# Block-causal attention and a token and channel mixer: u in one buffer, its float16 parts in two, with a new order

## Chip, cores and metric

The kernel runs on one core of a Trainium2 chip. The metric is the device time of one execution in microseconds. Engines: PE is the matrix engine (PEld its weight loads), DVE, ACT and POOL the vector, scalar and general engines, SP the engine whose queue issues all DMAs here.

## The reference

Eight batches of eight heads, 576 tokens, head size 64. The attention is masked by blocks of 64 tokens (a token sees its own block and those before). Its output, all heads beside each other, is x (8 x 576 x 512), and a mixer follows:

```python
theta = x @ w_theta
zr, zi = x * np.cos(theta), x * np.sin(theta)
y = np.einsum('ts,bsd->btd', w_tok_r, zr) + np.einsum('ts,bsd->btd', w_tok_i, zi)
u = x + y
return u + np.maximum(u @ w_ch, 0.0)
```

Inputs and outputs are float32. The kernel reaches that precision on PE by splitting operands into two 16-bit (or reduced float32) parts and adding three products: high by high, low by high, high by low.

## The kernel before

A pair p is two heads; four pairs make one batch b. For each pair the scores go into PSUM in three pieces (parts sab, sc, sd), DVE takes row maxima (m), ACT the exponentials (e), ACT and DVE split them into two float16 parts (high, low), a DMA transposes them (turn), PE multiplies with v (weighted), and DVE divides by the sums (normalise). Pairs 0 to 3 go another way: PE transposes the float32 exponentials (tp), ACT or DVE copies them (cp), and v is scaled in float32 (vf, the function v_scaled).

For each batch the mixer takes x through these parts: xh, xl, xt split and turn x; theta is a product on PE; turns, rest, size, sines make cosine and sine; z multiplies them with x; zh and zl are the float16 parts of z; mix is the token product on PE, 27 matmuls of 288 columns for each of 4 blocks of 128 channels (dt) and 2 halves of the tokens (th). The rest is about u:

- xs (add_parts, L837) adds the two x parts into u for two dt at once (dp 0 or 1), on DVE; xd (unscale, L841, run by the helper `times`, L319 on ACT and L323 on DVE) scales them;
- u (take_u, L845) adds the mix result from its PSUM bank, in place;
- uh (L851, helper) and ul (L856) make the float16 parts of u in the tile uhl;
- c (channel, L865) multiplies them with the channel weights, 12 matmuls for each of 4 dt (called e) and 2 halves;
- out (rectify, L871) adds the rectified result to u, in place; fin (unlift) rescales u, in place; store (L880) writes u out by a DMA from SP's queue.

u lies in two buffers, used by turns: `u_all[self.b % 2]`. uhl has one buffer. The first u buffer first holds the identity (`made_ident`), the second the float32 channel weights before they are split (L373). The uhl buffer first holds raw weights (L368).

The order is written out. Each part has its needs: `turn_of(tag, last, bufs)` hands a part the users of the buffer's former content. The list PLACES gives each part a place; `order_of` sorts the parts by it and asserts that all needs come first. Instructions are issued in that order, so each engine's queue follows it. Two needs matter here: mix of batch b needs all c of batch b-1 (L1059), and uh needs the last reader of its uhl buffer (L1050). ON names, with a letter for each instance, the engine of a part (P is POOL, D is DVE, A is ACT). BANKS gives the PSUM banks in the order in which parts take them: bank 0 is the attention output o, banks 1 to 7 go to scores, theta, mix (group y) and c. RUNNING places filler matmuls on ones (L1082): before the n-th part of the order, into a bank, so many.

Of the kernel before, what the change touches and what calls it, by code (L numbers as in the profile page):

```python
# [181 lines left out]


RUNNING = [
    (12, 0, 7), (25, 0, 13), (43, 0, 8), (63, 0, 3), (75, 0, 3), (336, 0, 3), (396, 3, 8), (404, 5, 2), (767, 1, 5)
]
ON = {"w5": "AAAAAAAAA",
      "wc": "PDDDPPPDP",
      "vc": "DPDPPPPDPDDPPPDPPPPPPPDP",
      "qh": "APPPPAPPPAPPPAAPAAAAPPPAPAAPPAAA",  # L190
      "vf": "PDDD",
      "cp": "DDDADDAADAAAADAA",
# [943 lines left out]
```

## Time and profile before

| what | value |
|---|---|
| median of 3 runs | 674.82 us (672.94 to 677.4) |
| the profiled execution | 670.92 us, of it 669.1 us span |
| PE, DVE, ACT, POOL busy | 97%, 86%, 79%, 26% of the span |
| granted clock of PE | 1.0 of full speed |

The profile shows one execution. The span runs from the first to the last instruction; busy is the time in which an engine had an instruction under way, and for PE the ends of matmuls are modelled, since they overlap. "Releaser" of an idle time is what ended it.

### The profile page before, as it was taken

What the parts mean: (1) busy time and instruction counts of PE and PEld (TensorE: products, weight loads), DVE (VectorE), ACT (ScalarE), POOL (GpSimd) and SP (SyncE); (2) the same over time, 40 slices, a digit from 0 to 9 for tenths busy, and PEclk for the clock granted to TensorE, in tenths of its full rate; (3) what the DMA queues carried; (4) which work ended last, traced back from release to release, by engine and by line L of the source; (5) the groups of instructions that cost most, each with busy time, mean ns of one, the idle gap of its engine ahead of it and who ended that gap; (6) DMA issues with size and microseconds to landing.
All of it is one profiled execution on the core that took longest, in us unless ns stands there. A gap on an engine that the chain in (4) does not pass through costs nothing.

```text
span 669.1 us, 17391 instructions
## 1 busy us (share of the span) xinstructions
PE 649.4 (97%) x7285; PEld 501.6 (75%) x7285; DVE 575.9 (86%) x844; ACT 531.5 (79%) x829; POOL 176.4 (26%) x214
## 2 busy tenths in 40 slices
PE   8899999999989999999999999999999999999997
PEld 4688856887658767887688867888678867886675
DVE  5999899899898989999999999889999999755534
ACT  5999798877898689896997699887898799737611
POOL 1302313211042004640072003340183003611600
PEclk9999999999999999999999999999999999999999
DMA  8871265998989977799779787879989753950101
GB/s 330 321 295 65 90 126 109 215 217 201 225 173 192 203 169 143 185 193 241 170 155 186 167 191 167 179 165 180 196 168 201 166 102 96 194 85 19 54 1 72
DMA packets 245854, 110.51 MB, mean 165 GB/s; under 512 B 227216, under 2 KB 227216, under 8 KB 245776
## 3 DMA queue, kind: packets, MB, share of 16 engines
q1 hardware_dynamic: 245776, 109.40, 72.9%
q8 instruction: 57, 0.93, 0.6%
q14 instruction: 21, 0.17, 0.1%
HBM read 43.06 MB, written 9.44 MB: 78 GB/s over the span
## 4 chain that ended last, share of the span: by engine, by line
PE 62%; ACT 14%; DVE 10%; DMA 8%; issue 3%; POOL 1%; SPq 0%; ACTq 0%; DVEq 0%; POOLq 0%
PE ps L832 25%; PE ps L763 10%; PE ps L865 9%; PE ps L673 9%; PE ps L589 7%; DMA pt<-p 5%; DVE m L623 4%; ACT t L627 3%; ACT p L319 2%; DMA q<-in_qT 2%; DVE p L654 2%; ACT aa L797 1%; ACT zh L317 1%; DMA w_raw<-in_w_theta 1%; PE ps L602 1%
## 5 line engine op out<-in xcount | busy, mean ns | idle before, releaser
L627 ACT ACTIVATE t<-ps,m 128x320 f32<-128x320 f32 (+4 forms) x320 | 149.1, 534 | 32.6 <-DVE m L623 23.8
L832 PE MATMUL ps<-wT_h,zh 128*128 128x288 f16 x540 | 154.7, 286 | 1.3 <-ACT t L627 0.9
L832 PE MATMUL ps<-wT_h,zl 128*128 128x288 f16 x540 | 154.4, 286 | 1.3 <-DVE zl L822 1.1
L832 PE MATMUL ps<-wT_l,zh 128*128 128x288 f16 x540 | 154.4, 286 | 0.0
L623 DVE TENSOR_REDUCE m<-ps 128x2 f32<-128x896 f32 (+4 forms) x160 | 125.0, 816 | 14.4 <-PE ps L594 9.0
L832 PEld LDWEIGHTS <-zh 128*128 128x128 f16 x1080 | 105.5, 98 | 27.4 <-issue 0.9
L673 PE MATMUL ps<-v,pt 128*128 128x65 f16 (+1 forms) x2760 | 114.2, 200 | 3.2 <-DMA pt<-p 1.3
L654 DVE SCALAR_TENSOR_TENSOR p<-t,p 128x1664 f16<-128x1664 f32 x56 | 105.6, 1898 | 6.2 <-ACT p L319 6.1
L865 PE MATMUL ps<-uhl,wch_h 128*128 128x288 f16 x512 | 95.3, 286 | 0.2 <-DVE u L871 0.2
L319 ACT ACTIVATE p<-t 128x1664 f16<-128x1664 f32 x56 | 88.3, 1606 | 2.8 <-DMA pt<-p 2.3
L673 PEld LDWEIGHTS <-pt 128*128 128x128 f16 x2520 | 82.1, 97 | 8.5 <-DMA pt<-p 3.8
L763 PE MATMUL ps<-wth_h,xt 128*128 128x512 f16 (+1 forms) x384 | 87.5, 345 | 0.1
L763 PEld LDWEIGHTS <-xt 128*128 128x128 f16 (+1 forms) x576 | 46.5, 102 | 44.7 <-issue 3.0
L865 PE MATMUL ps<-uhl,wch_l 128*128 128x288 f16 x256 | 73.2, 286 | 0.0
L832 PEld LDWEIGHTS <-zl 128*128 128x128 f16 x540 | 52.8, 98 | 15.8 <-DVE zl L822 2.0
L865 PEld LDWEIGHTS <-wch_h 128*128 128x128 f16 x512 | 48.6, 98 | 14.5 <-issue 1.3
L763 PE MATMUL ps<-wth_l,xt 128*128 128x512 f16 (+1 forms) x192 | 57.3, 344 | 0.0
L589 PE MATMUL ps<-k,qh 64*128 64x288 f32 (+3 forms) x384 | 50.0, 395 | 3.0 <-POOL qh L540 1.9
L809 POOL TENSOR_TENSOR aa<-aa,x_ring 128x512 f32<-128x512 f32 (+1 forms) x29 | 36.2, 1257 | 54.0 <-ACT aa L799 24.9
L589 PEld LDWEIGHTS ps<-k,qh 64*128 64x128 f32 x384 | 34.8, 189 | 16.7 <-issue 3.5
L845 DVE SCALAR_TENSOR_TENSOR u<-ps,gain,u 128x288 f32<-128x288 f32 x64 | 31.5, 511 | 17.1 <-PE ps L832 16.6
L822 POOL TENSOR_TENSOR zl<-aa,zh 128x512 f16<-128x512 f32 (+1 forms) x26 | 28.0, 1079 | 48.8 <-ACT zh L317 48.6
(165 smaller groups left out, 1150.6 us busy)
## 6 DMA issues: line engine op xcount, KB each, us to landing
raw_v<-in_v SPq DMA_DIRECT2D x32, 384.0 KB, 4.3
q<-in_qT SPq DMA_DIRECT2D x32, 320.0 KB, 3.6
k<-in_kT SPq DMA_DIRECT2D x32, 320.0 KB, 3.6
out<-u SPq DMA_DIRECT2D x32, 288.0 KB, 2.4
w_raw<-in_w_tok SPq DMA_DIRECT2D x5, 576.0 KB, 6.0
p<-in_w_tok SPq DMA_DIRECT2D x4, 576.0 KB, 6.0
w_raw<-in_w_theta SPq DMA_DIRECT2D x2, 512.0 KB, 6.4
p<-in_w_theta SPq DMA_DIRECT2D x2, 512.0 KB, 8.3
```

The source lines that it names most:

```text
L319: engine.mul(to, x, scale)
L589: nc.tensor.matmul(s[hh][:, col:col + n], lhsT=qq[rows, i * P:(i + 1) * P], rhs=kk[rows, k0:k0 + n], start=nn == 0 and (j == 0 or c == "ab ...
L623: nc.vector.tensor_reduce(out=m, in_=s, axis=AX.XY if i in (2, 3) else AX.X, op=ALU.max, negate=True)
L627: nc.scalar.activation(out=to, in_=s, func=AF.Exp, scale=1.0, bias=m)
L654: nc.vector.scalar_tensor_tensor(out=self.p[:, 1, :], in0=self.t, scalar=LIFT, in1=self.p[:, 0, :], op0=ALU.mult, op1=ALU.subtract)
L673: nc.tensor.matmul(o[:, i, :], lhsT=pp[:, block, :], rhs=vv[:, of, hh, :], start=nn == 0, stop=nn == n - 1)
L763: nc.tensor.matmul(g[rows, 0:cols.stop - cols.start], lhsT=x[:, dt, part, i, rows], rhs=ww[:, dt, cols], start=(n == 0), stop=(n == 11))
L809: engine_of("z", (2 * self.b + hf) * 5 + n).tensor_tensor(out=cd, in0=cd, in1=x, op=ALU.mult)
L822: engine_of("zl", (2 * self.b + hf) * 5 + n).tensor_tensor(out=zl, in0=cv, in1=zh, op=ALU.subtract)
L832: nc.tensor.matmul(g, lhsT=zz[:, kk, cols], rhs=ww[:, kk, ts], start=(n == 0 and kk == k0 and nn == 0), stop=(n == 4 and nn == 2))
L845: nc.vector.scalar_tensor_tensor(out=self.u(dt)[:, ts], in0=bank("y", self.b, dt, th)[:, 0:HS], scalar=g_y, in1=self.u(dt)[:, ts], op0=ALU ...
L865: nc.tensor.matmul(g[:, 0:HS], lhsT=ww[:, dt, e * P:(e + 1) * P], rhs=uu[:, dt, th * HS:(th + 1) * HS], start=(n == 0), stop=(n == 11))
```

## The change

u has one buffer for all batches. uhl has two, named uhl0 and uhl1, used by turns. The channel weights and the identity share the one u buffer, the raw weights take uhl0. Through `turn_of`, xs of batch b now needs the stores of batch b-1 instead of b-2 (batch 0 needs the last split of the channel weights), and uh of batch b needs c of batch b-2 instead of b-1. The rule that mix of batch b needs c of batch b-1 stays. PLACES, BANKS, RUNNING and parts of ON are written anew.

```diff
 RUNNING = [
-    (12, 0, 7), (25, 0, 13), (43, 0, 8), (63, 0, 3), (75, 0, 3), (336, 0, 3), (396, 3, 8), (404, 5, 2), (767, 1, 5)
+    (11, 0, 7), (24, 0, 12), (65, 0, 5), (78, 0, 2), (336, 0, 3), (381, 0, 5), (392, 1, 5), (399, 1, 2), (767, 1,
+    4)
 ]
 ON = {"w5": "AAAAAAAAA",
...
-      "qh": "APPPPAPPPAPPPAAPAAAAPPPAPAAPPAAA",
-      "vf": "PDDD",
-      "cp": "DDDADDAADAAAADAA",
+      "qh": "APAPPPPAAPPAPPAPPAAPPPPAPAAPPAPP",
+      "vf": "PPPP",
+      "cp": "DDDADAAAADAAAAAA",
...
-      "z": "DDDDDPDDPDPDDDDPPDDPDDPPPPDPPDPPDPDDDPDPPDPPDPPPPDDPPDDPDPDPDPPPPPPPPPPPDDPPDPPP",
+      "z": "PDPPDDPDDDPPDPPDDDPDDDPPPPPPDPPPDPPPDDDPPDPDPPDDPPPDPDDDDDPDPDPPPPDDDPPDDDPPDPDD",
...
-      "zl": "DPPPPPPDPDPDDDPPDDDPPPPPDPPPPDPPDDPDDDPDPDDDPPPPPDPPPDPPPPDPPPDPDDPDDPPDDDDPPPDP",
+      "zl": "PDPDPDPPPPPDDDPDPDDDPPDPPPDPPPPPPPDPPPDPDDPPPPPDPPDDPDPPPDPPDPPPDPPDDPPPPDDDPPP",
...
-      "xd": "DDADADAAAAADADAA",
+      "xd": "DDDDAAAAAAAADDAA",
       "uh": "AAAAAAAAAAAAAAAA",
-      "fin": "PDPDPPPPPAADADAPPPAPDADAADDDDDDPDAAAADD"}
+      "fin": "AAPDPDAAADAADDAAPAPADDPPPDDADDDDADDDDADP"}
...
-    u_all = [const.tile([P, NDT, S], F32, name=f"u{i}") for i in range(2)]
-    made_ident = u_all[0][:, 0, 0:P]
+    u_all = const.tile([P, NDT, S], F32, name="u_all")
+    made_ident = u_all[:, 0, 0:P]
...
-    raws = [mo.tile([P, 2, 2 * S], U32, tag="uhl", name="w_raw"),
+    raws = [mo.tile([P, 2, 2 * S], U32, tag="uhl0", name="w_raw"),
...
-            "ch": u_all[1][:, :, 0:DM]}
+            "ch": u_all[:, :, 0:DM]}
...
         def u_parts(self):
-            both = self.tile_of("uhl", [P, 2, NDT, S], F16)
+            both = self.tile_of(f"uhl{self.b % 2}", [P, 2, NDT, S], F16)
...
         def u(self, dt):
-            return u_all[self.b % 2][:, dt]
+            return u_all[:, dt]
...
     for dp in range(NDT // 2):
-        turn_of(f"u{dp}", [w_last["ch"][dp]], 2)
+        turn_of(f"u{dp}", [w_last["ch"][dp]])
...
-        u_free = turn_of("uhl", c_all)
+        u_free = turn_of(f"uhl{b % 2}", c_all)
         for dp in range(NDT // 2):
             two = (2 * dp, 2 * dp + 1)
-            free = turn_of(f"u{dp}", [("store", b, dt) for dt in two], 2)
+            free = turn_of(f"u{dp}", [("store", b, dt) for dt in two])
```

## Rows read from the trace of the kernel before

**Rows 1.** The page: the span, and busy us (share) xinstructions by engine.
```profile
span 669.1 us, 17391 instructions
...
PE 649.4 (97%) x7285; PEld 501.6 (75%) x7285; DVE 575.9 (86%) x844; ACT 531.5 (79%) x829; POOL 176.4 (26%) x214
```

**Rows 2.** Four stretches: length, busy us by engine, PE clock, DMA share, GB/s.
```profile
0.00:100.00 100.00, 90.91 (x772) 70.74 (x773) 86.26 (x135) 86.53 (x138) 21.89 (x61) 1.00 0.61 205
100.00:260.00 160.00, 154.72 (x1799) 115.14 (x1796) 144.67 (x212) 134.69 (x210) 29.19 (x34) 1.00 0.91 189
260.00:660.00 400.00, 398.67 (x4682) 311.88 (x4681) 342.39 (x493) 309.51 (x482) 124.81 (x120) 1.00 0.71 146
660.00:669.10 9.10, 5.07 (x42) 3.82 (x39) 2.57 (x6) 0.78 (x2) 0.51 (x1) 0.98 0.34 130
```

**Rows 3.** The chain that ended last, its tail: start us, us, what.
```profile
621.66 5.18 PE ps L763 x24
626.84 26.46 PE ps L832 x216
653.30 11.77 PE ps L865 x96
```

**Rows 4.** Tile uhl: what its engines' idle time ended with (us, times).
```profile
  DVE u L845: 16.5, 4
  ACT uhl L319: 5.0, 6
  DVE u L871: 0.2, 1
```

**Rows 5.** Waits of PE, one of them: us in total, times, longest.
```profile
PE ps L832 <- DVE u L871: 0.4, 1, 0.4
```

**Rows 6.** Tile u: count, ns min/median/max, first and last start; landing of stores last.
```profile
L837 DVE TENSOR_TENSOR u<-xt x16: 1342/1348/1355, 82.0 to 602.6; 128x1152 f32<-128x1152 f16 x16
L319 ACT ACTIVATE u<-u,gain x10: 1238/1257/1289, 144.9 to 604.0; 128x1152 f32<-128x1152 f32 x10
L323 DVE TENSOR_SCALAR u<-u,gain x6: 810/814/821, 83.4 to 554.5; 128x1152 f32<-128x1152 f32 x6
L425 DVE SCALAR_TENSOR_TENSOR wch_l<-u,size_ch,wch_h x2: 1274/1280/1285, 69.9 to 71.5; 128x1024 f16<-128x1024 f32 x2
...
DMA to landing us min/median/max: 2.1/2.4/6.8
```

**Rows 7.** Timelines of SP and DVE: stores and the next batch's first u.
```profile
348.86 2.32 SPq L880 DMA_DIRECT2D out<-u  x2
354.60 0.50 DVE L845 SCALAR_TENSOR_TENSOR u<-ps,gain,u 128x288 f32<-128x288 f32 x1
500.94 0.38 SPq L880 DMA_DIRECT2D out<-u  x1
509.94 0.52 DVE L845 SCALAR_TENSOR_TENSOR u<-ps,gain,u 128x288 f32<-128x288 f32 x1
575.82 0.57 SPq L880 DMA_DIRECT2D out<-u  x1
584.24 0.94 DVE L845 SCALAR_TENSOR_TENSOR u<-ps,gain,u 128x288 f32<-128x288 f32 x2
```

**Rows 8.** Lines 569 and 809: count, ns min/median/max, first and last start.
```profile
L569 DVE TENSOR_SCALAR v<-raw_v,sizes x3: 611/612/612, 30.1 to 48.7; 128x768 f32<-128x768 f32 x3
L569 POOL TENSOR_SCALAR v<-raw_v,sizes x1: 1895/1895/1895, 25.4 to 25.4; 128x768 f32<-128x768 f32 x1
L809 DVE TENSOR_TENSOR rr<-rr,x_ring x16: 675/692/1783, 100.6 to 631.6; 128x512 f32<-128x512 f32 x16
```

**Rows 9.** The page's groups: shapes, count, busy us and mean ns, idle before.
```profile
L654 DVE SCALAR_TENSOR_TENSOR p<-t,p 128x1664 f16<-128x1664 f32 x56 | 105.6, 1898 | 6.2 <-ACT p L319 6.1
L319 ACT ACTIVATE p<-t 128x1664 f16<-128x1664 f32 x56 | 88.3, 1606 | 2.8 <-DMA pt<-p 2.3
```

More of the change, by code (lines that the diff above doesn't have):

```diff
@@ L32 @@
 PLACES = [
[135 rows of a table removed]
[135 rows of a table added]
 ]
 BANKS = [
[11 rows of a table removed]
[11 rows of a table added]
 ]
 RUNNING = [
-    (12, 0, 7), (25, 0, 13), (43, 0, 8), (63, 0, 3), (75, 0, 3), (336, 0, 3), (396, 3, 8), (404, 5, 2), (767, 1, 5)
+    (11, 0, 7), (24, 0, 12), (65, 0, 5), (78, 0, 2), (336, 0, 3), (381, 0, 5), (392, 1, 5), (399, 1, 2), (767, 1,
+    4)
 ]
 ON = {"w5": "AAAAAAAAA",
-      "wc": "PDDDPPPDP",
-      "vc": "DPDPPPPDPDDPPPDPPPPPPPDP",
-      "qh": "APPPPAPPPAPPPAAPAAAAPPPAPAAPPAAA",
-      "vf": "PDDD",
-      "cp": "DDDADDAADAAAADAA",
-      "n0": "DDADDDDDADDAAAAADDDDDDDADADAAAAAADADADDDAAADADADDADDADADDADDADDA",
+      "wc": "DDPDPPPDD",
+      "vc": "PDPPDPDPPDPDPPDPPDPPPDPP",
+      "qh": "APAPPPPAAPPAPPAPPAAPPPPAPAAPPAPP",
+      "vf": "PPPP",
+      "cp": "DDDADAAAADAAAAAA",
+      "n0": "DDDADDADDDAAADDAADDDDDAAADDDADDAADDADDDDDDDDAADADDAAAAAAADDAADAD",
       "v1": "DDDDAAAAAAAAAAAAAAAAAAAAAAAAAAAA",
       "high": "DDDDDDDDAAAAAAAAAAAAAAAAAAAAAAAAAAAAAAAAAAAAAAAAAAAAAAAAAAAAAAAA",
-      "kh": "DDDDDDDDDDDDDDDDPPAPAPAPPAPAPPAA",
+      "kh": "DDDDDDDDDDDDDDDDPAPPAPAPPAPAPAAP",
       "kl": "DDDDDDDDDDDDDDDDDDDDDDDDDDDDDDDD",
@@ L199 @@
       "xl": "DDDDDDDDDDDDDDDDDDDDDDDDDDDDDDDDDDDDDDD",
-      "z": "DDDDDPDDPDPDDDDPPDDPDDPPPPDPPDPPDPDDDPDPPDPPDPPPPDDPPDDPDPDPDPPPPPPPPPPPDDPPDPPP",
+      "z": "PDPPDDPDDDPPDPPDDDPDDDPPPPPPDPPPDPPPDDDPPDPDPPDDPPPDPDDDDDPDPDPPPPDDDPPDDDPPDPDD",
       "zh": "AAAAAAAAAAAAAAAAAAAAAAAAAAAAAAAAAAAAAAAAAAAAAAAAAAAAAAAAAAAAAAAAAAAAAAAAAAAAAAAA",
-      "zl": "DPPPPPPDPDPDDDPPDDDPPPPPDPPPPDPPDDPDDDPDPDDDPPPPPDPPPDPPPPDPPPDPDDPDDPPDDDDPPPDP",
+      "zl": "PDPDPDPPPPPDDDPDPDDDPPDPPPDPPPPPPPPDPPPDPDDPPPPPDPPDDPDPPPDPPDPPPDPPDDPPPPDDDPPP",
       "xs": "DDDDDDDDDDDDDDDD",
-      "xd": "DDADADAAAAADADAA",
+      "xd": "DDDDAAAAAAAADDAA",
       "uh": "AAAAAAAAAAAAAAAA",
-      "fin": "PDPDPPPPPAAADADAPPPAPDADAADDDDDDPDAAAADD"}
+      "fin": "AAPDPDAAADAADDAAPAPADDPPPDDADDDDADDDDADP"}
 WHOLE = 4
@@ L713, in u_parts @@
         def u_parts(self):
-            both = self.tile_of("uhl", [P, 2, NDT, S], F16)
+            both = self.tile_of(f"uhl{self.b % 2}", [P, 2, NDT, S], F16)
             return [both[:, i] for i in range(2)]
         def u(self, dt):
-            return u_all[self.b % 2][:, dt]
+            return u_all[:, dt]
         def u_two(self, dp):
-            return u_all[self.b % 2][:, 2 * dp:2 * dp + 2]
+            return u_all[:, 2 * dp:2 * dp + 2]
         def rows(self, dt, i0, ni):
@@ L850, in u_high @@
             ts, two = slice(th[0] * HS, (th[0] + 1) * HS) if th else slice(0, S), slice(2 * dp, 2 * dp + 2)
-            times(engine_of("uh", self.b * 2 + dp), self.u_parts()[0][:, two, ts], u_all[self.b % 2][:, two, ts], w_down["ch"])
+            times(engine_of("uh", self.b * 2 + dp), self.u_parts()[0][:, two, ts], u_all[:, two, ts], w_down["ch"])
         def u_low(self, dp, *th):
@@ L855, in u_low @@
             ts, two = slice(th[0] * HS, (th[0] + 1) * HS) if th else slice(0, S), slice(2 * dp, 2 * dp + 2)
-            nc.vector.scalar_tensor_tensor(out=ul[:, two, ts], in0=u_all[self.b % 2][:, two, ts], scalar=w_down["ch"],
+            nc.vector.scalar_tensor_tensor(out=ul[:, two, ts], in0=u_all[:, two, ts], scalar=w_down["ch"],
                                            in1=uh[:, two, ts], op0=ALU.mult, op1=ALU.subtract)
@@ L923, in attention_phase_mixer @@
     for tag, last in (("zh", [("wm", "theta")]), ("zl", [("wm", "tok")]), ("aa", w_last["theta"]), ("rr", w_last["tok"]), ("xt0", w_last["tok"]), ("xt1", w_last["tok"]),
-                      ("uhl", [("w", n, 3) for n in range(0, len(todo), 2)]), ("p0", [("w", n, 3) for n in range(1, len(todo), 2)]),
+                      ("uhl0", [("w", n, 3) for n in range(0, len(todo), 2)]), ("p0", [("w", n, 3) for n in range(1, len(todo), 2)]),
                       ("p1", [("w", n, 3) for n in range(1, len(todo), 2)])):
```

292 rows, old and new, of tables (BANKS, PLACES) are left out of this document.

## The prediction

> **What bounds the kernel now.** First the page's busy shares, then the same by stretches. PE is busy for 649.4 of 669.1 us, DVE for 575.9 [rows 1]. Over the span that says PE; by stretches it says where [rows 2]. Up to 100 us, while the weights are split and the first pairs have no mixer beside them, PE is idle for 9.1 us, and ACT and DVE are each busy for some 86 of 100 us. From 100 to 260 us PE is idle for 160 - 154.72 = 5.3 us, from 260 to 660 us for 400 - 398.67 = 1.3 us. The last 9 us are the final rectifications and stores, 4.0 us of them without PE. So an order can give back little: 6.6 us in the 560 us of the body, and part of the beginning.
>
> Then the chain that ended last. Its tail is PE alone, back to back: theta of batch 7 behind the c matmuls of batch 6, then 216 mix matmuls in 26.46 us (0.1225 us each), then 96 c matmuls [rows 3]. A dependency costs time only where it stops that row of matmuls.
>
> Then the tiles that the change touches. Whatever reads or writes uhl sat idle 16.5 us for DVE's u, 5.0 us for ACT's uhl, 0.2 us for DVE's rectified u: nothing on that list is L865, the matmuls that read the old parts [rows 4]. So the one uhl was never waited for. The list of waits has PE's mix matmuls standing for u once, 0.4 us [rows 5].
>
> **The change part by part.**
>
> *uhl twice.* It removes the wait of uh(b), the high part, for the c matmuls of batch b-1. Both kernels keep another rule, that mix(b) follows c(b-1) on PE, and uh(b) needs u(b), which needs mix(b). The removed wait is always over before the kept one, and [rows 4] shows none. Worth 0; a gain is excluded by that order.
>
> *u once.* xs(b), the sum of the x parts, now waits for the stores of batch b-1 (of its two dt) instead of b-2. Per batch that puts one chain between those stores and the first u(b): landing, xs, xd, u. Prices: landing 2.1 / 2.4 / 6.8 us (least, median, most), xs 1.35 us on DVE, xd 1.26 us on ACT or 0.81 on DVE [rows 6]. So 2.4 + 1.35 + 1.26 = 5.0 us at the median, 6.8 + 1.35 + 1.26 = 9.4 at worst. How much room is there? I read from the timelines when the last store of a batch is issued and when the next batch's first u starts. The narrowest three [rows 7]: batch 2 to 3, 348.86 (its dt 1, the first of the row's two; the other half's xs comes later) to 354.60, 5.7 us; 4 to 5, 500.94 to 509.94, 9.0 us; 5 to 6, 575.82 to 584.24, 8.4 us. The other four are 10 us and more. In the tail c(6) ends at 621.66 and the mix of batch 7 runs from 626.84 to 653.30 [rows 3]: wide enough. At the median landing all fit, the narrowest with 0.7 us over; at the worst the shortage is 3.7 + 0.4 + 1.0 = 5.1 us in all. Besides, sorting the parts by PLACES puts xs of the first half just ahead of its u in the batches from 2 on (in the order xs(3) is part 1448, its u 1468; before, xs came 162 to 310 parts ahead). xd is on ACT for batches 2 to 5 and 7, so DVE's u now stands behind a trip DVE, ACT, DVE, five times. Behind that u in DVE's queue are low parts and row maxima, on which the transposes and PE's scores wait; and a y bank stays taken until u reads it. What hides it: 7 banks turn beside the one of o, and PE fills the next while u is late. If the cover holds always, 0; if never, five times 1.26 = 6.3 us. The rows are nearer to cover ([rows 5]), so I take one trip of five: **+1.3 us**.
>
> *u as the place of the channel weights.* xs(0) must now wait for the low parts of w_ch, the last of which starts at 71.5 us and takes 1.28; the first xs ran at 82.0 [rows 6]. Cost 0 while this order holds, and the new order keeps the two that way; below 0 is excluded, since a wait is added. The identity is made in u and copied out before any weight: 0.
>
> *Order, banks and engines anew.* The work is the same. The filler matmuls (L1082) fall from 52 to 45; at the tail's 5.18 us for 24 matmuls of 512 columns, 0.216 us each, that is 1.5 us of PE [rows 3], but they stand where PE would wait anyhow: between -1.5 and 0, taken 0. v_scaled goes to POOL for pairs 1 to 3, 1.90 us instead of 0.61 [rows 8]: three times 1.28 = 3.9 us if each is on the path, 0 if DVE's relief pays for it; taken 0, because up to 100 us DVE is as full as ACT [rows 2]. Of the other moves, POOL gets five zl and three qh and gives four z and four fin; DVE gives, with v_scaled, ten operations and takes seven; I price both as even, and the order's bounds below hold what is wrong with that. But POOL beside DVE is not free: the same DVE product rr takes 0.675 us at least, 0.69 at the median, 1.78 at most [rows 8]. By this row a collision costs 1.1 us and meets fewer than half of the products. The Trainium skill ("SBUF — State Buffer", Who interferes with whom) has a rule for it: a VectorE instruction with two SBUF inputs and a GpSimd one that reads SBUF exclude each other for a whole instruction. By that rule the three v_scaled could stop DVE for 3 x 1.90 = 5.7 us in place of the 1.8 us that it did itself, 3.9 us more as an estimate; by the row it is one or two collisions.
>
> The order itself I can only bound. Below: all of the body's 6.6 us of idle PE, and some 3 us of the beginning, -10. Above: if 260 to 660 us went as 100 to 260 did, 5.3 / 160 x 400 - 1.3 = +11.9. I take 0, nearer to the stretch in which PE hardly waits.
>
> Sum, against the profiled execution's own 670.92 us (span 669.1 and 1.8 around it): 670.9 + 0 + 1.3 + 0 + 0 = 672.2. That execution is 3.9 us below the median of the runs, 674.82; on the median it is 676.1, so **676 us**.
>
> **The rivals.** About 1% (6.7 us) is what a measurement of this kernel can tell from no change, so the edges are 668.1 and 681.6.
>
> Slower: the new chain store, xs, xd, u is late in most batches, y banks stay taken, and PE stops. Place: the first u of batches 2 to 7. Price: 5.1 us for late landings, and at each of the five trips half of the op that may be ahead in each queue, a low part on DVE (1.90) and a p cast on ACT (1.61) [rows 9], 1.75 us, 8.8 in all; 13.9 us of lateness. Four held y banks leave three, and a pair's first scores take four, so PE pays all of it where scores are next and none where mix can go on; I take 10: 674.8 + 10 = 685. It decides once PE pays over 6.7. For it: from 100 us on, DVE is busy 487 of 560 us, so it has no room to wait. Against it: [rows 5].
>
> Faster: the order is better, and DVE gets slack. Half of the body's idle PE goes (3.3 us) and a third of the 13.5 us in which ACT idles in the first 100 us (4.5 us): 674.8 - 7.8 = 667. For it: DVE has three operations fewer. Against it: 1.3 us of idle PE in the last 400 us can't give more.
>
> POOL in DVE's way: the three v_scaled on POOL stop DVE, or stand on the path themselves, at 1.28 us each, in the first 100 us, and all is passed on: 676.1 + 3.9 = 680.0. For it: DVE is near full there. Against it: a median product is not slowed [rows 8].
>
> The change does not do what it says: uhl twice frees nothing. I hold that as part of the likeliest case.
>
> **How the numbers follow.** The likeliest (the chain fits, order even) 0.47 and its own range 670 to 680; POOL in DVE's way 0.08, which lies within 1% too; slower by the chain or by a worse order 0.25; faster 0.20. That makes 0.20, 0.55, 0.25. The range leaves out a tenth on each side: below, 665 is the faster case with 2 us more; above, 687 is the order's bound, 674.8 + 11.9.
>
> **What would show it.** uh should never wait for L865, as before. xs (L837) should start within a few us after a store lands, and DVE should show waits for DMA out<-u of under 5 us in all; more, or PE waiting for DVE u (L845) or its queue for over 3 us, speaks for the slower rival. Idle PE from 100 to 260 us well under 5.3 us speaks for the faster one; a first mix matmul some 4 us later for POOL in DVE's way. The tail should still run 26.5 us of mix without a gap. I am wrong if the first 100 us move by more than 4 us, which nothing here prices.

## The result and the profile after

The kernel after takes 676.78 us (median of 20 runs, 673.1 to 681.59), the kernel before in the same rounds 673.18 (20 runs, 669.79 to 678.32). The ratio is 1.0052 with a 95% interval of [1.0035, 1.007]: 3.5 us slower, a small loss clear of the noise, within 1%. The forecast was 676.0, between 665 and 687, with no change beyond 1%. Four single runs below (three of before, one of e12) fell into a slower state, with granted clocks of 0.981 to 0.984; the ratios and the fit leave them out.

The profiled execution of after is the longest of its runs, 681.59 us with a span of 679.8, 4.8 us over the median, as that of before was below its own. So the two pages are 10.7 us apart where the medians are 3.6 apart, and the first thing to find is which of the 10.7 belong to the kernel. Line numbers of after are one higher than those of before, and tile u is called u_all.

Page of after: the span, PE's and DVE's busy time, and the granted clock of TensorE by slices of 17 us (9 is full):

```profile
span 679.8 us, 17405 instructions
...
PE 657.2 (97%) x7278; PEld 509.3 (75%) x7278; DVE 581.2 (85%) x844; ACT 536.6 (79%) x828; POOL 183.1 (27%) x215
...
PEclk9799899999999999999999999998999999999999
```

The four stretches of after (length, busy us of PE, PEld, DVE, ACT, POOL, then clock, DMA share, GB/s), against [rows 2]:

```profile
0.00:100.00 100.00, 90.15 (x648) 71.29 (x648) 76.39 (x121) 81.92 (x133) 20.21 (x61) 0.93 0.59 198
100.00:260.00 160.00, 155.08 (x1826) 115.61 (x1825) 145.90 (x207) 136.12 (x213) 33.11 (x36) 1.00 0.90 188
260.00:660.00 400.00, 396.22 (x4682) 310.08 (x4680) 349.21 (x498) 315.26 (x479) 129.26 (x118) 1.00 0.73 148
660.00:679.80 19.80, 15.73 (x129) 12.33 (x126) 9.67 (x20) 3.28 (x5) 0.51 (x1) 0.95 0.16 60
```

In the first 100 us PE is as busy as before (90.15 to 90.91), but it got 648 matmuls done and not 772, at a mean clock of 0.93 and not 1.00. (Part of that is the other order: a second execution of after, below, did 725 at 0.98.) From 100 to 260 us it is idle for 4.9 us (before 5.3), from 260 to 660 us for 3.8 (before 1.3; in the second execution of after 2.7). So the profiled loss has two places: the beginning, by the clock, and the long body, by 2.5 us of idle PE in this execution.

PE's waits in after (us in total, times, longest):

```profile
PE ps L674 <- DMA pt<-p: 5.0, 5, 1.7
...
PE ps L603 <- ACT t L628: 2.0, 1, 2.0
PE ps L603 <- DVE r L683: 1.8, 1, 1.8
```

In before, PE waited 1.3 us for pt (the transposes of the softmax rows by DMA), 1.1 us for ACT's t at this line, and not for r. No wait of PE in after is for u. The line of before for pt, and the one thing that DVE's u waited for in after, the mix matmuls:

```profile
PE ps L673 <- DMA pt<-p: 1.3, 2, 0.8
```

```profile
DVE u_all L846 <- PE ps L833: 12.8, 11, 2.8
```

Tile uhl, what its engines' idle time ended with, and the tail of the chain that ended last (start, us, what):

```profile
  DVE u_all L846: 20.0, 6
  ACT uhl L320: 2.6, 4
```

```profile
640.34 23.63 PE ps L833 x192
663.97 11.77 PE ps L866 x96
```

The c matmuls (L866) are not among what uhl waited for, as in [rows 4], and the tail is the PE-bound one of [rows 3].

### The profile page after: what moved, and what is told of

It reads as the page before. It is cut to its first block, busy times and chain, and to the rows that moved or that the text cites. A ratio compares the mean times of both kernels' runs of the same rounds, so it can differ in the third digit from the quotient of the medians.

```text
span 679.8 us, 17405 instructions
## 1 busy us (share of the span) xinstructions
PE 657.2 (97%) x7278; PEld 509.3 (75%) x7278; DVE 581.2 (85%) x844; ACT 536.6 (79%) x828; POOL 183.1 (27%) x215
## 4 chain that ended last, share of the span: by engine, by line
PE 66%; ACT 14%; DMA 12%; DVE 4%; issue 2%; SPq 1%; POOL 0%; ACTq 0%
PE ps L833 24%; PE ps L866 11%; PE ps L674 10%; PE ps L764 9%; PE ps L590 8%; DMA pt<-p 8%; ACT t L628 3%; ACT aa L798 2%; ACT zh L318 2%; DMA w_raw<-in_w_tok 1%; ACT p L320 1%; DMA raw_v<-in_v 1%; PE ps L640 1%; DVE m L624 1%; ACT aa L786 1%
## 5 line engine op out<-in xcount | busy, mean ns | idle before, releaser
L628 ACT ACTIVATE t<-ps,m 128x576 f32<-128x576 f32 (+4 forms) x320 | 148.4, 528 | 32.4 <-DVE m L624 18.2
L624 DVE TENSOR_REDUCE m<-ps 128x2 f32<-128x384 f32 (+4 forms) x160 | 125.2, 816 | 15.9 <-PE ps L595 14.1
L674 PE MATMUL ps<-v,pt 128*128 128x65 f16 (+1 forms) x2760 | 117.8, 202 | 7.1 <-DMA pt<-p 5.0
L866 PE MATMUL ps<-uhl,wch_h 128*128 128x288 f16 x512 | 95.5, 286 | 0.0
L674 PEld LDWEIGHTS <-pt 128*128 128x128 f16 x2520 | 82.9, 98 | 14.3 <-DMA pt<-p 6.7
L866 PE MATMUL ps<-uhl,wch_l 128*128 128x288 f16 x256 | 73.2, 286 | 0.0
L866 PEld LDWEIGHTS <-wch_h 128*128 128x128 f16 x512 | 48.5, 98 | 14.9 <-issue 0.8
L810 POOL TENSOR_TENSOR aa<-aa,x_ring 128x512 f32<-128x512 f32 (+1 forms) x29 | 37.7, 1312 | 72.1 <-ACT aa L798 41.3
L541 POOL TENSOR_SCALAR qh<-q 128x640 f32<-128x640 f32 (+1 forms) x20 | 15.3, 767 | 117.0 <-PE ps L603 69.9
L823 POOL TENSOR_TENSOR zl<-aa,zh 128x512 f16<-128x512 f32 (+1 forms) x31 | 34.5, 1118 | 33.0 <-ACT zh L318 32.8
```

Source lines behind the costliest of these rows:

```text
L541: engine.tensor_scalar(out=out, in0=x, scalar1=scale, scalar2=0.0, op0=ALU.mult, op1=ALU.add)
L624: nc.vector.tensor_reduce(out=m, in_=s, axis=AX.XY if i in (2, 3) else AX.X, op=ALU.max, negate=True)
L628: nc.scalar.activation(out=to, in_=s, func=AF.Exp, scale=1.0, bias=m)
L674: nc.tensor.matmul(o[:, i, :], lhsT=pp[:, block, :], rhs=vv[:, of, hh, :], start=nn == 0, stop=nn == n - 1)
L810: engine_of("z", (2 * self.b + hf) * 5 + n).tensor_tensor(out=cd, in0=cd, in1=x, op=ALU.mult)
L823: engine_of("zl", (2 * self.b + hf) * 5 + n).tensor_tensor(out=zl, in0=cv, in1=zh, op=ALU.subtract)
```

## The beginning: one kernel, two executions

Theory A was that after's beginning is what costs: PE stands near 24 us, the granted clock falls behind it, and everything later shifts. Theory B was that the single u is late. Theory C was that the new order of the body costs. The kernel after was profiled a second time, beside other kernels and on one chip with them:

> The kernel after, unchanged, beside the three others on the same chip. If its distance to before is what the first runs gave, the ratio is 1.003 to 1.007; a ratio of 1.000 to 1.002 would say that part of that distance was not in the kernel. Theory 'the beginning is slow in every execution': first mix matmul at 113 us; theory 'only in some, where the granted clock falls': 107 to 110 us in a faster execution.

Measured: 676.34 us (12 runs), ratio 1.0056 [1.003, 1.0081], so the distance to before repeats. Its profiled execution has a span of 674.2, near its median. The beginnings of the two executions, first the longest one: ACT's and PE's timelines (start, us, engine, line, operation, idle before), then two stretches as above.

```profile
23.26 1.25 ACT L406 ACTIVATE w_val<-w_raw 128x1152 f32<-128x1152 f32 x1 [1.34 <-DMA w_raw<-in_w_tok]
...
25.72 0.48 PE L603 MATMUL ps<-k,qh 64*128 64x64 f32 x4 [1.96 <-ACT t L628]
26.13 6.66 PE L674 MATMUL ps<-v,pt 128*128 128x65 f32 x30
```

```profile
25.00:30.00 5.00, 4.28 (x22) 4.17 (x23) 4.90 (x10) 5.00 (x11) 0.00 (x0) 0.60 0.46 123
30.00:35.00 5.00, 5.00 (x26) 5.00 (x26) 1.51 (x5) 1.66 (x4) 0.46 (x2) 0.50 1.00 403
```

The same lines in the second execution (e8):

```profile
21.63 1.25 ACT L406 ACTIVATE w_val<-w_raw 128x1152 f32<-128x1152 f32 x1
...
24.08 0.44 PE L603 MATMUL ps<-k,qh 64*128 64x64 f32 x4 [0.51 <-ACT t L628]
24.45 3.56 PE L674 MATMUL ps<-v,pt 128*128 128x65 f32 x30
```

```profile
25.00:30.00 5.00, 4.63 (x42) 4.40 (x42) 4.83 (x12) 4.84 (x11) 0.46 (x2) 1.00 0.74 246
30.00:35.00 5.00, 5.00 (x46) 4.80 (x45) 4.76 (x8) 5.00 (x7) 0.90 (x1) 1.00 1.02 409
```

In the first, the raw token weights landed late; ACT's widening of them waited 1.34 us with the exponentials of pair 1 behind it in ACT's queue, PE stood 1.96 us, and after that stand the granted clock was 0.60 and then 0.50, the lower of the two levels. Thirty matmuls of L674 took 6.66 us there, which in the second execution, and in before, took 3.56 us at full clock. The first mix matmul came at 113.21 us. In the second execution the weights had landed, PE stood 0.51 us, the clock held, and the first mix matmul came at 107.35, against 106.26 in before. So 5.9 us of the profiled 10.7 lie between two executions of the same code. They begin at this landing and are complete by 64 us, where the same matmuls start at 63.69 and at 57.83. In two more kernels with this beginning, e5 and e6 below, PE stood 1.79 and 1.85 us at the same place, and the first mix matmul came at 110.4 and 110.2: the late landing is not rare.

The two were compared with what follows by landmarks on PE: the first mix matmul, and the time from there to the end of the last one ("body"). What comes after is 15.8 us in each of them.

```
profiled execution                       first mix     body
before                                      106.26   547.05
e1, after's order, before's buffers         107.31   549.54
e8, the kernel after                        107.35   551.03
after                                       113.21   550.76
e7, before's buffers, xs and xd moved       107.93   565.89
e2, the same with one u                     109.13   567.13
```

## The order and the single u taken apart

**e1: the order alone.** Order, banks, fillers and engines of after, with u twice and its parts once.

```diff
-    u_all = const.tile([P, NDT, S], F32, name="u_all")
+    u_all = [const.tile([P, NDT, S], F32, name=f"u{i}") for i in range(2)]
...
-            both = self.tile_of(f"uhl{self.b % 2}", [P, 2, NDT, S], F16)
+            both = self.tile_of("uhl", [P, 2, NDT, S], F16)
```

> The changed kernel's order, banks, fillers and engines, but the buffers of before: u twice, its parts once. Theory A (the beginning: in the new order PE idles for 2 us near 24 us, its granted clock falls to 0.5 and the first 110 us get longer): as the changed kernel, ratio to before 1.004 to 1.007, some 676.8 us. Theory B (the single u: u comes late behind the stores): the loss goes, 0.999 to 1.001. Theory C (the new order of the body, above all late transposes near 467 and 524 us): as A, 1.004 to 1.007.

Measured: 674.48 us (12 runs), ratio 1.0015 [0.999, 1.0039]. That is nearest to theory B's range, and below those of A and C. So the order costs about 1.0 us by itself, at most 2.6, and after's distance of 3.5 us would leave some 2.5 for the buffers; but the two ratios come from different chips, and the fit below puts most of that down to the clock. By the landmarks the order loses 1.05 us up to the first mix and 2.5 in the body; of these 3.5 us, some 2 are that before's profiled execution (670.92) lies below its median (673.18), while that of e1 lies at its own. Where in the body: PE's waits of e1, then DVE and SP ahead of one of them (timelines).

```profile
PE ps L673 <- DMA pt<-p: 4.9, 5, 1.6
```

```profile
505.35 1.35 DVE L837 TENSOR_TENSOR u<-xt 128x1152 f32<-128x1152 f16 x1
...
507.88 1.35 DVE L837 TENSOR_TENSOR u<-xt 128x1152 f32<-128x1152 f16 x1
509.14 2.09 DVE L654 SCALAR_TENSOR_TENSOR p<-t,p 128x1664 f16<-128x1664 f32 x1
...
511.38 8.93 SPq L658 DMA_TRANSPOSE pt<-p  x2
```

The wait for pt is 3.6 us longer than in before, and as long as in after, in an order that puts both xs of a batch on DVE shortly ahead of the low part of p; the transpose can't be issued before that part is there, and PE then stands 1.6 us at 517. That the two xs are what delays it is read from the timeline; it wasn't tried. DVE's u waits here for the same thing as in after, and as long:

```profile
DVE u L845 <- PE ps L832: 13.1, 13, 2.8
```

The body of e8 is 1.5 us longer than that of e1, which has the same order with u twice. Two stretches of e8 at a lower clock, from 515 to 525 us (shown further down), account for up to 5 x 0.12 + 5 x 0.22 = 1.7 us, an estimate from their granted clocks. So these profiles show no body time that the single u costs beside the clock.

**e2 and e7: xs and xd moved in the old order.** One u forces xs of batch b behind the stores of batch b-1. e2 is the kernel before with one u, its parts twice, and one move: xs and xd of batches 1 to 7 to some 25 parts ahead of the first u of their half. That is later than one u forces, for most halves: xs(2, 1) could follow the last store of its buffer, part 1077, and is part 1239. e7 has the same order, with the buffers of before.

```diff
 order of parts, e2 and e7, for b = 1 to 7 and dp = 0, 1
-xs(b, dp) xd(b, dp) ... store(b-1, 2*dp + 1) ... u(b, 2*dp)
+store(b-1, 2*dp + 1) ... xs(b, dp) (6 parts) xd(b, dp) ... u(b, 2*dp)
 buffers, e2 alone
-    u_all = [const.tile([P, NDT, S], F32, name=f"u{i}") for i in range(2)]
+    u_all = const.tile([P, NDT, S], F32, name="u_all")
```

> The order of before with u once and its parts twice; only xs and xd of batches 1 to 7 are moved behind the stores that they now wait for, some 25 parts ahead of the first u. Theory A: 0.999 to 1.002. Theory B: 1.004 to 1.007, with waits of DVE for the stores or of PE for u. Theory C: 0.999 to 1.002.

> The kernel before, u twice and its parts once, with the order of e2_u_once_only: xs and xd of batches 1 to 7 moved to some 25 parts ahead of the first u, nothing else. It tells apart what costs the 21 us of e2_u_once_only. If the cost is the place of xs and xd in the queues of DVE and ACT, where the rest of the order left no room for them: 685 to 694 us here as well. If it is the wait of xs for the stores, which only one u brings: 672 to 677 us here.

Measured: e2 694.1 us (6 runs), ratio 1.0308 [1.0269, 1.0347]; e7 691.55 us (6 runs), ratio 1.0282 [1.0249, 1.0314]. None of the three theories had e2 slower by 3%. So 19 of e2's 21 us come from where this order puts xs and xd, with both buffers of u free, and one u adds 2.5 us by the medians, 1.7 by the ratios, on different chips. The intervals of the ratios overlap. What the earliest place that one u allows would cost in this order was not run. In e2 a wait for the stores is seen on DVE:

```profile
DVE u_all L837 <- DMA out<-u_all: 1.1, 1, 1.1
```

PE's waits in e7 show where the 19 us go:

```profile
PE ps L832 <- ACT t L627: 5.5, 3, 2.6
PE ps L832 <- DVE zl L822: 4.7, 5, 2.1
...
PE ps L589 <- DVE u L845: 1.7, 2, 1.3
...
PE ps L832 <- DVE u L845: 1.3, 1, 1.3
PE ps L832 <- POOL xt L822: 1.2, 1, 1.2
```

By these waits the sums take the time on DVE and ACT in which the z parts, the exponentials and u itself were due; PE waits for these, and never for a store. By the body column e7 loses 18.8 us and e2 20.1. In the new order, where the rest was arranged around late sums, a like move is in e1, which loses 1.0 us in all.

## The other parts of the change

**e5: the parts of u once again,** all else as in after. **e6: v_scaled of pairs 1 to 3 on DVE again.**

```diff
 e5
-            both = self.tile_of(f"uhl{self.b % 2}", [P, 2, NDT, S], F16)
+            both = self.tile_of("uhl", [P, 2, NDT, S], F16)
 e6
-      "vf": "PPPP",
+      "vf": "PDDD",
```

> The kernel after with its float16 parts of u held once again, so that u and its parts are both held once; order, banks and engines of after. Theory 'the second uhl is worth nothing': no wait of uh for the c matmuls (L866), the time within 1.5 us of the kernel after on the same chip, no loss against it. Rival 'the second uhl is what makes one u bearable': uh waits for L866, its u bank frees later, and the time is 3 to 8 us above the kernel after.

> The kernel after with v_scaled of pairs 1 to 3 on DVE again, as before. Theory 'POOL in DVE's way, or v_scaled on the path' (the prediction's rival): the first mix matmul comes 3 to 4 us earlier than in the kernel after and the time falls by as much. Theory 'they stand beside other work': the time within 1.5 us of the kernel after; DVE takes 1.8 us more, which nothing waits for.

Measured: e5 676.02 us, ratio 1.0044 [1.0023, 1.0066]; e6 675.76 us, ratio 1.004 [1.0014, 1.0065]; after beside them 1.0056 (12 runs each). Neither can be told from after. The first mix matmul of e6 came at 110.2, 3.0 us ahead of that in after's longest execution, as the rival had it, but 2.9 behind that of e8, and the time did not fall with it. In e5 tile uhl waits for the same two things as in after:

```profile
  DVE u_all L845: 19.9, 6
  ACT uhl L319: 2.6, 4
```

The second uhl buys nothing in this order. And v_scaled on POOL does not cost what I had priced. Its line in after, and beside it POOL and DVE of e7, which has the beginning of before:

```profile
L570 POOL TENSOR_SCALAR v<-raw_v,sizes x4: 905/907/908, 22.3 to 53.8; 128x768 f32<-128x768 f32 x4
```

```profile
25.89 1.89 POOL L569 TENSOR_SCALAR v<-raw_v,sizes 128x768 f32<-128x768 f32 x1
...
25.45 1.55 DVE L414 SCALAR_TENSOR_TENSOR w_val<-w_raw,w_val 128x1152 uint32<-128x1152 uint32 x1
```

All four take 0.91 us in after. The 1.90 of [rows 8] was one instruction, begun while DVE ran a step with two inputs in SBUF: in e7 it begins 0.44 us behind that step, and from the step's end, 27.00, to its own, 27.78, pass 0.78 us, near the 0.91 of a free one. By these rows it stood still behind DVE. The Trainium skill ("SBUF — State Buffer", Who interferes with whom) states that between two such instructions the one that is issued first holds the other for its whole length; these rows agree.

## Attempts on the beginning

**e3: the old beginning.** After, with its first 404 parts in before's order, banks and engines. **e4: more fillers.** After with 22 more filler matmuls (L1083): 5 ahead of sc(1), 9 ahead of sd(1), 8 ahead of sd(3).

```diff
 e3
-order of parts 0 to 403: as in after
+order of parts 0 to 403: as in before
 e4, RUNNING
-    (65, 0, 5), (78, 0, 2)
+    (65, 0, 10), (78, 0, 11), (243, 1, 8)
```

> The changed kernel, but its first 404 parts (up to the scores of pair 6, just ahead of the first mix) in the order, with the banks, fillers and engines, of before. Theory A: the loss goes, 0.998 to 1.002, some 3.5 us less than the changed kernel, with the clock at 1.0 up to 100 us. Theory B: 1.004 to 1.007. Theory C: 1.004 to 1.007.

> The changed kernel with 22 filler matmuls more in the beginning: 5 ahead of sc of pair 1, 9 ahead of sd of pair 1, 8 ahead of sd of pair 3, where PE idled for 1.0, 2.0 and 1.8 us. Theory A, if the lower clock is the price and not the idle time itself: 1.000 to 1.003, the clock never at 0.5 up to 100 us, the first 30 weighted matmuls 3.6 us instead of 6.6. Theories B and C: 1.004 to 1.007, whatever the clock does there. Fillers in the way of real matmuls would make it 1.007 and more.

Measured: e3 682.19 us (6 runs), ratio 1.013 [1.0093, 1.0167]; e4 678.98 us (12 runs), ratio 1.0086 [1.0061, 1.0111]. e3 says little: it reached its first mix matmul at 106.12, as before did, and then stood at the seam, where the new body wants its z parts earlier than the old beginning gives them:

```profile
110.23 0.42 PE L832 MATMUL ps<-wT_h,zl 128*128 128x288 f16 x1 [3.82 <-POOL zl L822]
```

e4 kept the clock at 1.00 up to 60 us (0.98 from there to 65), and lost it then all the same (stretches as above, then PE's timeline):

```profile
0.00:65.00 65.00, 59.33 (x454) 46.45 (x455) 50.54 (x80) 55.30 (x88) 13.15 (x42) 1.00 0.69 256
65.00:70.00 5.00, 5.00 (x30) 3.77 (x29) 2.80 (x6) 2.11 (x5) 2.67 (x3) 0.67 0.34 90
```

```profile
63.84 2.62 PE L1083 MATMUL ps<-ones 128*128 128x512 bf16 x8 [1.97 <-ACT t L628]
```

The eight fillers ahead of sd(3) themselves stood 1.97 us for ACT's t, so they ran behind that stand and did not fill it. Its first mix matmul came at 109.5, later than the 107.35 of the second execution of after, and the kernel is 2.3 us slower than after by the ratios. 22 fillers at 0.216 us are 4.8 us of PE, so they cost as if half of them stood on the path. So e4 does not tell what a filled stand would be worth there.

**e9 to e12: the widening of the token weights later.** (w(2,1) is ACT's step of that widening, w(2,2) and w(2,3) are DVE's two; w(8,2) and w(8,3) are those of the last channel weights.) In e9 it stands behind the exponentials that it stood ahead of on ACT. e10 moves DVE's normalise of head 5 ahead of the last channel weights too, behind which PE waited 1.8 us for r. e11 is e10 with before's buffers. e12 is e9 with the two DVE steps of the widening also behind the row maxima of pair 1.

```diff
 order of parts
 e9
-w(2,1) e(1,1,3) w(2,2) e(1,1,2) qh(2) w(2,3) e(1,0,3) w(3,1) m(1,4) m(1,0)
+e(1,1,3) e(1,1,2) qh(2) e(1,0,3) w(2,1) w(2,2) w(3,1) m(1,4) w(2,3) m(1,0)
 e10, e11 besides
-w(8,2) w(8,3) ... normalise(5)
+normalise(5) w(8,2) w(8,3)
 e12
+e(1,1,3) e(1,1,2) qh(2) e(1,0,3) w(2,1) w(3,1) m(1,4) m(1,0) w(2,2) w(2,3)
```

> The kernel after with one move: the widening of the first token weights (w_val<-w_raw, L406, and the two DVE steps behind it) stands behind the exponentials and the qh that it stood ahead of. In five of six profiled executions with after's beginning PE was busy 2.1 to 3.5 us between 20 and 25 us; where it was 2.1 to 2.8, w_raw had landed late, ACT waited 1.2 to 1.3 us for it, PE stood 1.8 to 2.0 us for the exponentials behind, and the granted clock fell to 0.5 to 0.67 from 25 to 35 us; first mix matmul at 110 to 113 us instead of 107.4. Theory 'a late landing costs after its slower executions': no wait of over 0.7 us for ACT t (L628) near 23 us, clock 1.00 from 20 to 40 us, the mean of the runs' clocks above 0.995 (after 0.994), the time 1 to 2 us under after's ratio of 1.0052 to 1.0056, so 1.002 to 1.004. Theory 'the clock is not what costs': ratio 1.005 again.

> e9 and a second move: normalise of head 5 (r, its reciprocal, x_ring; L683 to L689) goes ahead of the narrowing of the last channel weights (u_all, 0.69 and 1.22 us on DVE), behind which PE's first scores of pair 3 stood 1.76 us near 61 us, before a granted clock of 0.66 to 0.77 in the 5 to 10 us behind. Theory 'stalls of the first 100 us, and the clock behind them, are most of what after lost beside the single u': clock 1.00 from 60 to 75 us, first mix matmul under 106.5 us, ratio 0.999 to 1.002. Theory 'the single u and the body are': ratio within 0.001 of e9's.

> e10 with the buffers of the kernel before (u twice, its parts once); the order of e10. The single u as a cost of its own: after stood 1.0052 to 1.0056 against e1_order_only's 1.0015 with the same order, so e11 is to be 1 to 2.7 us under e10 if the single u costs the same wherever it stands. If the difference between after and e1 came only from the beginnings of their executions, e11 and e10 agree within 0.7 us. It may also be the version that is faster than both: ratio 0.996 to 0.999.

> The kernel after, its one u and its parts twice, with the widening of the first token weights behind the exponentials on ACT (as in e9_w_behind) and now the two DVE steps behind it after the row maxima of pair 1 as well. In e9 those two steps stood ahead of two maxima in DVE's queue: DVE waited 1.74 us for ACT's w_val, PE 2.02 us for the exponentials behind, and the granted clock still fell to 0.53 between 30 and 35 us. Theory 'the stall near 24 us and the clock behind it cost the difference': no PE wait of over 0.7 us between 20 and 30 us, clock 1.00 from 20 to 40 us, ratio 1.001 to 1.004. Theory 'the beginning costs the same wherever its work stands': ratio 1.005 to 1.008, as after, e9 and e10.

Measured (12 runs each): e9 678.07 us, 1.0085 [1.0067, 1.0103]; e10 677.82, 1.0079 [1.006, 1.0099]; e11 677.51, 1.0063 [1.0038, 1.0087]; e12 675.48, 1.0049 [1.0026, 1.0071]. None is better than after by more than its interval, and e11, which might have been faster than both, is slower than before. e11 is under e10 by 0.3 us by the medians and by 1.1 by the ratios, so it does not decide between a single u without a price of its own (under 0.7) and one with it (1 to 2.7). e9 moved the stand instead of removing it (DVE's and PE's timelines, and a stretch):

```profile
25.38 0.76 DVE L412 TENSOR_SCALAR w_val<-w_val 128x1152 uint32<-128x1152 uint32 x1 [1.74 <-ACT w_val L405]
...
29.15 4.29 PE L639 MATMUL ps<-ident_r,t 128*128 128x128 f32 x18 [2.02 <-ACT t L627]
```

```profile
30.00:35.00 5.00, 5.00 (x27) 4.68 (x25) 4.03 (x8) 5.00 (x8) 0.46 (x2) 0.53 1.02 400
```

e10 kept that stand (2.10 us) and did not take away the next one: with r ahead of the channel weights PE stood the same 1.76 us, now for ACT's t, the clock was 0.77 and 0.89 from 65 to 75 us, and the first mix matmul came at 110.1, not under 106.5. So r does not seem to be the only thing that this stand waits for:

```profile
65.83 0.44 PE L602 MATMUL ps<-k,qh 64*128 64x64 f32 x4 [1.76 <-ACT t L627]
```

Back to e9: with the widening later on ACT, DVE's own steps of it waited 1.74 us with row maxima behind them, and PE stood 2.02 us for the exponentials of those. e12 mends that. In its profiled execution PE's longest wait between 20 and 30 us is 1.0 us near 22 us (for ACT's pt, as in e8), over the mark of 0.7, and 0.8 follows near 31; but the long one for the exponentials is gone (0.5 is left), and the clock is 1.00 from 20 to 40 us:

```profile
25.00:30.00 5.00, 4.51 (x40) 4.20 (x39) 4.37 (x8) 5.00 (x10) 0.00 (x0) 1.00 0.37 95
30.00:35.00 5.00, 4.19 (x38) 3.95 (x37) 4.93 (x8) 4.19 (x6) 0.46 (x2) 1.00 0.99 394
```

Yet the ratio stays at 1.0049, where theory A wanted 1.001 to 1.004. Theory A is not borne out, though the interval, from 1.0026, reaches into its range: the stand near 24 us made one execution long, but a kernel that avoids it in its profile is not faster by more than the noise.

## What the distance of 3.5 us is made of

Every run has a mean granted clock of its execution. Within a kernel its runs differ mostly by that: one slope for all, fitted to 240 runs with a height for each kernel and round, is 0.55 us for 0.001 of clock, and leaves 0.87 us of a spread of 1.74. With it the means of each kernel are brought to the same clock of 1.000 (the first 20 runs of before have no clock on record and are not among them):

```
kernel                        runs   mean us   mean clock   at clock 1.000
before                          95    672.71       0.9973      671.2 +- 0.1
e1, order alone                 12    674.67       0.9953      672.1 +- 0.2
after (with e8)                 32    676.24       0.9938      672.9 +- 0.2
e5, parts once                  12    675.81       0.9940      672.5 +- 0.2
e6, v_scaled on DVE             12    675.39       0.9952      672.7 +- 0.3
e12                             11    675.65       0.9944      672.6 +- 0.2
e7, sums moved                   6    691.47       0.9960      689.3 +- 0.3
e2, sums moved, one u            6    694.46       0.9935      690.9 +- 0.2
```

Of the 3.5 us between the means of before and after, the order has 0.8 (671.2 to 672.1), the single u 0.8 (to 672.9, with an error of 0.3), and 1.9 us are the lower clock, 0.0035 of it. e2 against e7 gives the single u 1.6 us at equal clock, e10 against e11 (673.5 and 673.9) nothing; so its own price is 0 to 1.6 us. Part of such differences may be the chip: before itself lies at 671.6 on the one of e1 and e2, and at 671.1 on the other three. Against before on its own chip, e1 loses 0.4 us and e8 1.4, and e2 1.1 more than e7. This is a fit and not an experiment.

Where the clock is lost is seen in profiled executions only: in those of after, e8, e1, e5, e6 and e9 to e12 it is near 25 to 30, 65, 470 and 515 us, each time behind a stand of PE. The last one in e8 (stretches, as above):

```profile
515.00:520.00 5.00, 3.38 (x54) 2.93 (x51) 4.86 (x9) 5.00 (x10) 4.41 (x4) 0.88 1.10 166
520.00:525.00 5.00, 5.00 (x61) 3.99 (x60) 2.16 (x5) 2.28 (x5) 0.72 (x1) 0.78 0.34 70
```

This stand is one of the waits for pt that came with the order. Behind the same wait the clock fell in e5 and e12 too, and held at 1.00 in after's longest execution, e1, e6, e9, e10 and e11. So the stands are in the kernel, and whether one costs the clock as well differs from execution to execution. That the four places make up the 1.9 us is likely and not shown: no kernel without all of them was run.

## Why the prediction was right, and where it was not

- **uhl twice: 0.** Right. uh never waits for L866 in after, and e5 is not slower without it.
- **One u: +1.3 us.** The cover is right: the trip from store to u fits. DVE has no wait for out<-u in after's profile and 0.5 us in e8 (the line below), under the 5 us that I had set as the mark, and PE has none for u. The size, 0 to 1.6 us at equal clock, agrees with 1.3 and with 0; that one trip of five is uncovered, from which the 1.3 came, is seen in no profile.

```profile
DVE u_all L838 <- DMA out<-u_all: 0.5, 1, 0.5
```

- **w_ch in u, fillers: 0.** No wait for the weights by xs is in the lists. What the seven fillers less are worth was not run by itself; fillers are not free to add: 22 more cost 2.3 us.
- **v_scaled on POOL: 0 to 3.9, taken 0.** The value taken is right, and the bound was mis-sized: I read 1.90 us from a single instruction that had stood behind DVE. Free of that it takes 0.91, so the difference to DVE's 0.61 is 0.9 us for three, not 3.9. The rival "POOL in DVE's way" falls with e6. The count behind DVE's slack is wrong: DVE gives ten operations and takes not seven but ten, with one more each in the wc, vc and n0 of ON, and the pages have 844 instructions of DVE in both kernels, with 575.9 us before and 581.2 after. So the argument for the faster rival did not hold.
- **Order: -10 to +11.9, taken 0.** Measured +1.0 for e1, inside. But the 0 is the difference of two large numbers, and the working didn't see that: moving the sums close to u, as in e7, costs 19 us if nothing else moves, and the new order of the rest has nearly all of it back. My bound from above, 11.9, would not have held without that. The body's idle PE went from 1.3 to 3.8 us (2.7 in e8), and PE's waits for transposes from 1.3 to 5.0 us (4.5 in e8).
- **The slower rival, 685.** It named the first u as late behind stores, with banks that stay taken. Its effect exists in e7, dearer than priced, by another way: the sums displace z parts and exponentials in the queues of DVE and ACT. The point from which it decides, 6.7 us of PE, is passed there and not in after.
- **The mark for being wrong:** that the first 100 us move by more than 4 us. In the profiled execution they did, the first mix matmul by 6.95; in a second execution of the same kernel by 1.09. The mark was set on a quantity that moved by 5.9 us between two executions of the same code, and the term that no step of the sum has is the granted clock: about half of the distance. The tail's 24 + 192 mix matmuls run in 2.94 + 23.63 us, as forecast, with 24 theta matmuls between them (1.43 us).

So no change beyond 1% is right, and so are the second uhl and the cover of the trip. That 676.0 is within 0.8 us of the measured 676.78 is in part luck: the forecast added 1.3 us to 674.82, the median of three runs of before, which lies 1.6 us above the 673.18 of 20 runs. The change itself was forecast as +1.3 us and is +3.5, with about 1 us of order and a term of 1.9 us, the clock, that the sum does not have; both are small beside the range.

## What to carry to other kernels

Price a step that a smaller buffer forces to a later place by the queue that it is put into, not by its own wait: here the wait was worth 0 to 2.5 us and the place 19, until the rest was arranged anew. Take no price from a single instruction without a look at what the neighbouring engine did beside it. Before explaining a difference between two profiles, profile the same kernel again: 5.9 us of the 10.7 here lay between two executions of the same code. And a wait has the name of what came last: when e10 moved that out of the way, the stand stayed as long, for the next thing.

## What the runs showed of the hardware

PE stood for 1.7 to 2.1 us, with short runs of matmuls around it, and the granted clock then was down to 0.5 to 0.67 for 5 to 10 us (after, e5, e6, e9 to e11); with 0.5 us in the same place (e8) it stayed at 1.00. A stand of like length did not always cost the clock: in the waits for pt near 520 us, of 1.6 to 1.9 us, it stayed at 1.00 in six of nine profiled executions. A stand that is short in itself cost 3.1 us more in the next thirty matmuls. And POOL's TENSOR_SCALAR of 128x768 takes 0.91 us or 1.89, nothing between, in the profiles of all the kernels here: 1.89 or 1.90 in the four with before's beginning, where it begins beside the same step of DVE each time.
